# Norms on the residual rows in SBUF, operand splits woven between output projections, fewer DMAs: an attention and GLU block on one core

## The chip, the core and the metric

The kernel runs on one core of a Trainium2 chip. A core has a matrix engine (TensorE, PE, with its weight loads as PEld), a vector engine (VectorE, DVE), a scalar engine (ScalarE, ACT), GpSimd (POOL) and SyncE (SP), which here only issues DMAs. ACT issues DMAs too, in its own order of instructions. The metric is the device time of one execution in microseconds (us). What a measurement of this kernel can tell from no change is about 0.5%, some 4.4 us.

## What is computed

A block of batch 1, sequence 2048 and width 512: a conditioned layer norm, "infini" attention (32 heads of 16, four segments of 512 rows, each with causal softmax inside the segment and a linear-attention memory of the segments before), an output projection with residual, a second conditioned layer norm, and a bilinear GLU of width 1376 with residual:

```python
mod = silu(c) @ w_mod                      # six vectors: sa, ca, ga, sb, cb, gb
h = layernorm(x) * (1 + ca) + sa
q, k, v = heads(h @ wq), heads(h @ wk), heads(h @ wv)
for s in range(4):                         # segments of 512 rows
    p = softmax(q_s @ k_s.T * scale + mask)
    a_mem = phi(q_s) @ M / (phi(q_s) @ z + 1e-6)
    o_s = g * a_mem + (1 - g) * (p @ v_s)
    M, z = M + phi(k_s).T @ v_s, z + sum(phi(k_s))
x = x + ga * (concat(o) @ wo)
h = layernorm(x) * (1 + cb) + sb
out = x + gb * ((h @ w_gate) * (h @ w_up) @ w_down)
```

## The kernel before

**Stages.** The first 500 us are the attention. Its work is cut into 32 half-groups (one of four segments, four heads); `v` counts them, and a loop over `v` from -2 to 32 runs five slots in each step. In a slot stand, in the program's order: `q_step` (TensorE makes transposed scores `q`, and VectorE takes their maximum into `nm`, for the row maxima of a later step), in one slot `av_step` (exponentials times values, `tb`), `fill()`, and `k_step` (TensorE makes the scores `k`, ACT takes their exponential into `pt`, GpSimd zeroes what the mask excludes). The tile of scores is used again one slot later, so the scores of a slot wait for the exponential of the slot before. Once in a step `n_step` turns the maxima: they are transposed by TensorE (`ntp`), copied by VectorE to `nt` (32 rows of 128) and put by DMA on two spare rows of the query tile `qst`, so that the next step's scores come out with the maximum subtracted. Every VectorE instruction recorded by a wrapper has line 40, matmuls line 90, transposes line 93.

**The filling.** `fill()` advances generators that hold the work which is not scores: first `fill_a` (projections to queries, keys and values, the memory), then `fill_b`: the output projections of segments 0 to 2, the norm ahead of the GLU and the first GLU weights. A generator yields what it has put down; a credit of `rate * share` per slot stops the filling, and `yield False` ends the slot's filling at once. `weave(a, b, at)` advances `b` once after each listed step of `a`.

**Output projection.** Segment outputs were stored to HBM by an earlier stage (`od`, four groups of 128x512 per segment). `wo_load` loads them (tiles `orl`), `wo_op` splits each into a rounded part `oH` (ACT) and a rest, which stays in the `orl` tile (VectorE). `wo_mm` makes, for each 128-row tile of the segment, twelve matmuls (`wops`: high, rest and weight rest for four groups) and `wo_add` adds them to the residual rows `xr`, which `xr_load` has loaded, and stores the sum to HBM (`x1d`). `lnC` loads the sums again (`x<-x1d`), takes the norm (`bn_stats`, mean and variance, one `tensor_scalar` per tile) and transposes them (`ctp`) into what the GLU reads. The product of the GLU's weights is prepared by `prep`: loads of w_gate and w_up (tile `w`), sums on GpSimd, a rounded part `AH` by ACT and a rest `AL`.

**What sets the order.** TensorE and VectorE take the program's order here. ACT's and SP's order comes from the tile scheduler; SP issues one DMA after another, and one that waits for a buffer or for an earlier transfer holds all behind it. After 544 us comes the GLU, in two halves of the rows.

Of the kernel before, what the change touches and what calls it, by code (L numbers as in the profile page):

```python
# [9 lines left out]
F32 = mybir.dt.float32  # L10
# [8 lines left out]
P = 128  # L19
# [39 lines left out]
def tile_kernel(ctx, tc, x, wq, wk_, wv, wo, beta, w_gate, w_up, w_down, c, w_mod, out):  # L59
# [147 lines left out]
    def ln(pool, hpool, xt, s, sc, sh, pfx, hb, fast, kept_h=None):  # L207
# [5 lines left out]
        for d in range(KT):  # L213
            h = pool.tile([P, L], F32, tag="hf", name=f"{pfx}hf{s}_{d}", bufs=hb[2])
            ln_col(bank(f"{pfx}tp{s}_{d}"), h, xt, d, sc, sh, A)
            hi = hpool.tile([P, L], F32R, tag=hb[0].format(d), name=f"{pfx}hH{s}_{d}", bufs=hb[1])
            lo = hpool.tile([P, L], F32R, tag=hb[0].format(4 + d), name=f"{pfx}hL{s}_{d}", bufs=hb[1])
            if fast:
                V.tensor_copy(hi, h)
                V.tensor_sub(lo, h, hi.bitcast(F32))  # L220
            else:
                act.activation(hi, h, AF.Copy)
                nc.gpsimd.tensor_sub(lo, h, hi.bitcast(F32))  # L223
            hH.append(hi)
            hL.append(lo)
            if kept_h is not None:
                kept_h.append(h)
            yield 0.45
            if not first and d % 2 == 1:
                yield False  # L230
# [71 lines left out]
    def n_step(u):  # L302
# [6 lines left out]
        for i in range(2):  # L309
            nc.scalar.dma_start(Q[96 + i:97 + i].rearrange("p h (q t) -> p (h q) t", t=P), nt[16 * i:16 * i + 16])  # L310
# [116 lines left out]
    def prep(i, key, pool, nb, rpool, rb, ce=nc.gpsimd, le=nc.gpsimd, step=False):  # L427
# [3 lines left out]
        for src, k0, j in ((w_gate, 0, 0), (w_gate, 2, 1), (w_up, 0, 7), (w_up, 2, 2)):  # L431
            pin(nc.sync.dma_start(w[:, j, :, 0:n], src.rearrange("(k p) f -> p k f", p=P)[:, k0:k0 + 2, f0:f0 + n]))
# [34 lines left out]
    def wo_load(s, pool):  # L467
        rw = []
        for g in range(NG - 2 if s == NSEG - 1 else NG):
            a = pool.tile([P, L], F32, tag="orl", name=f"orl{s}_{g}", bufs=4)  # L470
            pin(nc.sync.dma_start(a, od[s][g]))
            rw.append(a)
        return rw
# [24 lines left out]
    def both(a, b):  # L498
        while True:
            x, y = next(a, None), next(b, None)  # L500
            if x is None and y is None:
                return
            yield 0.0

    def paced(a):
        for _ in a:
            yield False

    def xr_load(s, pb, ts=range(4), tag="xr"):
        xrs = []  # L510
        for t in ts:
            xr = pb.tile([P, D], F32, tag=tag, name=f"xr{s}_{t}", bufs=4)
            pin(nc.sync.dma_start(xr, x[rows(s, t), :]))
            xrs.append(xr)
        return xrs
# [13 lines left out]
    def wo_mm(s, us, xrs, ts=range(4)):  # L529

        for t, xr in zip(ts, xrs):
            ps = bank(f"wops{s}_{t}")
            yield from wo_row(ps, t, us, range(NG))
            wo_add(s, t, xr, ps)

    def lnC(s, pool, hpool, xpool, tag, nb):
        xt = []
        for t in range(4):
            a = xpool.tile([P, D], F32, tag=tag, name=f"x1_{s}_{t}", bufs=nb)
            nc.sync.dma_start(a, x1d[s][t])  # L540
            xt.append(a)
        yield 0.1
# [4 lines left out]
        for d in (0, 2, 1, 3):  # L547
# [3 lines left out]
            if d > 1:  # L551
                yield False
# [367 lines left out]
    us = [[], [], []]  # L920

# [33 lines left out]
    def fill_a():  # L955
# [5 lines left out]
        for s in range(NSEG):  # L961
# [4 lines left out]
            for g in range(2 if s == 0 else 0, NG):  # L966
# [17 lines left out]
                if s == NSEG - 1 and g == 1:  # L984
                    xr0 = xr_load(0, pa, (0, 1), "x")
# [3 lines left out]
                if s == NSEG - 1 and g == NG - 1:  # L989
                    yield from weave(Q, ready, (0, 1, 2, 3))  # L990
                    memq.append(a_mem(s, g))
# [121 lines left out]
    for v in range(-2, NQ + 1):  # L1113
        rate[0] = 5.8 if v < 20 else 5.2
        on, prev = 0 <= v < NQ, 0 <= v - 1 < NQ
        for slot in range(5):
# [10 lines left out]
            if v == NQ and slot == 0:  # L1127
                assert B["orl_free"]
                o3 = wo_load(3, B["pb"])
                xr3 = xr_load(3, B["pb"])  # L1130
            if v == NQ and slot == 2:
                btag[:] = ["ms", "lq0", "ms", "lq1"]
                for f in (fa, fb):
                    for _ in f:
                        pass
                us3 = []
# [162 lines left out]
    for q in range(2):  # L1299
# [42 lines left out]
        if q == 0:  # L1342
            def rows_of(s, tags):
                r = []
                for t, (tg, nb) in enumerate(tags):
                    a = wpool.tile([P, D], F32, tag=tg, name=f"xn{s}_{t}", bufs=nb)
# [6 lines left out]
            def norms():  # L1353
                for s, tags in ((2, [("orl", 4)] * 4), (3, [("wor", 2)] * 2 + [("orow", 2)] * 2)):
# [156 lines left out]
```

## Time and profile before

| | |
|---|---|
| time, median of 3 runs (least to most) | 879.39 us (879.31 to 883.21) |
| the profiled execution: its own time, its span | 881.91 us, 879.8 us |
| TensorE busy | 832.8 us (95%) |
| VectorE busy | 650.6 us (74%) |
| ACT busy | 472.5 us (54%) |
| GpSimd busy | 424.1 us (48%) |
| moved by DMA | 139.46 MB, 159 GB/s over the span |

The span runs from the first to the last recorded instruction; the execution's own time holds some 2 us around it. In a row of the timeline stand start, duration, engine, line, operation, tiles and shapes, and in brackets the idle time before it on its engine with what ended that. In a table of stretches stand, for each, the busy time and count of every engine, then the granted TensorE clock (1.00 is full), the busy share of the DMA engines and their rate. "ACTq" and "SPq" are the issue queues of ACT and SP.

### The profile page before, as it was taken

How to read it: one execution, taken by the hardware profiler on the slowest of the kernel's cores; microseconds unless marked ns; L12 is line 12 of the kernel's file. 1: busy time of each engine (PE TensorE's matmuls, PEld its weight loads, DVE VectorE, ACT ScalarE, POOL GpSimd, SP SyncE). 2: the span in 40 equal slices, each digit the busy share in tenths (PEclk: the TensorE clock that was granted, in tenths of full speed). 3: DMA queues.
4: the chain of work that ended last, by engine and by line, in shares of the span. 5: the costliest groups of instructions: out<-in, count | busy, mean ns of one | idle time of the engine just before them, and what ended most of it. 6: DMA issues, size and time to landing. Idle time of an engine off the chain costs nothing.

```text
span 879.8 us, 14406 instructions
## 1 busy us (share of the span) xinstructions
PE 832.8 (95%) x4824; PEld 583.0 (66%) x4824; DVE 650.6 (74%) x1728; ACT 472.5 (54%) x740; POOL 424.1 (48%) x564
## 2 busy tenths in 40 slices
PE   8998999989999989999978899999999999999998
PEld 5765565555565656655644567788778888887886
DVE  7697677986778868788888759898784856666532
ACT  3757667777677766777554664333363523333321
POOL 4545546546455665486352533987200846550000
PEclk9999899999999999999999999999999999999999
DMA  7774456665648665677695552543414232212032
GB/s 236 225 235 159 146 160 201 214 209 174 207 142 252 199 190 157 220 234 239 209 285 177 160 180 97 176 146 105 163 30 127 87 120 64 56 55 93 0 118 96
DMA packets 112667, 139.46 MB, mean 159 GB/s; under 512 B 20112, under 2 KB 71312, under 8 KB 112592
## 3 DMA queue, kind: packets, MB, share of 16 engines
q1 hardware_dynamic: 106368, 130.91, 48.7%
q10 hardware_dynamic: 6224, 7.62, 2.4%
q8 instruction: 38, 0.62, 0.3%
q14 instruction: 37, 0.30, 0.1%
HBM read 87.48 MB, written 50.76 MB: 157 GB/s over the span
## 4 chain that ended last, share of the span: by engine, by line
PE 66%; DVE 13%; DMA 8%; ACT 5%; POOL 4%; issue 3%; ACTq 1%; SPq 0%; POOLq 0%; DVEq 0%
PE g L90 23%; PE acc L90 14%; PE tb L90 5%; DVE q L40 5%; PE k L90 5%; PE q L90 5%; PE vps L90 4%; PE kps L90 3%; PE qps L90 2%; ACT pt L330 2%; DMA xr<-in_x_dram 2%; PE wops L90 2%; POOL ahL L223 1%; DVE x L40 1%; DVE nm L40 1%
## 5 line engine op out<-in xcount | busy, mean ns | idle before, releaser
L40 DVE CUSTOM_DVE_ANT_0 q<-q,cmask 128x384 f32<-128x384 f32 (+3 forms) x512 | 246.7, 508 | 66.4 <-PE q L90 56.4
L330 ACT ACTIVATE pt<-k 128x1024 f32<-128x1024 f32 x160 | 163.8, 1024 | 68.7 <-PE k L90 47.3
L333 POOL TENSOR_SCALAR_AFFINE_SELECT pt<-pt 128x256 f32<-128x256 f32 (+1 forms) x224 | 105.4, 484 | 174.3 <-ACT pt L330 173.9
L90 PE MATMUL q<-kst,qst 96*128 96x384 bf16 (+3 forms) x512 | 102.1, 301 | 11.7 <-DVE nm L40 10.4
L90 PE MATMUL k<-qst,kst 98*128 98x384 bf16 (+3 forms) x512 | 97.9, 303 | 11.6 <-ACT pt L330 10.7
L448 POOL TENSOR_TENSOR w<-w 128x256 f32<-128x256 f32 (+1 forms) x84 | 72.0, 869 | 55.7 <-DMA w<-in_w_up_dram 38.2
L443 POOL TENSOR_TENSOR AL<-w,AH 128x512 fp32r<-128x512 f32 (+1 forms) x42 | 58.2, 1388 | 48.0 <-ACT AH L439 46.8
L90 PE MATMUL tb<-pt,v 128*32 128x512 f32 (+3 forms) x1024 | 76.2, 438 | 0.2 <-POOL pt L333 0.2
L90 PEld LDWEIGHTS <-kst 98*128 98x128 bf16 x512 | 38.8, 99 | 56.6 <-issue 48.4
L40 DVE DVE_READ_ACCUMULATOR2_ANT nm<- 128x1 f32 x512 | 72.3, 141 | 0.0
L90 PEld LDWEIGHTS <-qst 96*128 96x128 bf16 x512 | 43.6, 98 | 39.1 <-issue 14.4
L439 ACT ACTIVATE AH<-w 128x512 fp32r<-128x512 f32 (+3 forms) x88 | 46.8, 565 | 33.6 <-POOL w L448 20.5
L1453 DVE TENSOR_TENSOR mL<-mid,mH 128x512 fp32r<-128x512 f32 (+1 forms) x44 | 32.9, 751 | 41.4 <-ACT mH L1452 39.4
L90 PE MATMUL acc<-DH,mL 128*128 128x512 f32 x144 | 56.6, 393 | 0.9 <-DVE mL L1453 0.9
L90 PE MATMUL acc<-DH,mH 128*128 128x512 f32 x144 | 57.2, 397 | 0.0
L90 PE MATMUL acc<-DL,mH 128*128 128x512 f32 x144 | 56.5, 393 | 0.0
L90 PEld LDWEIGHTS tb<-pt,v 128*32 128x32 f32 x1024 | 28.7, 110 | 39.5 <-issue 35.9
L1452 ACT ACTIVATE mH<-mid 128x512 fp32r<-128x512 f32 (+1 forms) x44 | 27.1, 627 | 51.7 <-PE acc L90 50.1
L1245 ACT ACTIVATE p<-g 128x512 f32<-128x512 f32 (+1 forms) x22 | 13.1, 597 | 73.2 <-PE g L90 73.1
L443 DVE TENSOR_TENSOR AL<-w,AH 128x512 fp32r<-128x512 f32 (+3 forms) x44 | 29.2, 671 | 19.1 <-ACT AH L439 18.2
L359 ACT ACTIVATE tsb<-tb 128x512 f32<-128x512 f32 x32 | 19.1, 596 | 35.0 <-PE tb L90 33.4
L90 PE MATMUL g<-chH,AH 128*128 128x512 f32 (+1 forms) x88 | 34.8, 395 | 0.7 <-ACT p L1245 0.7
(286 smaller groups left out, 2060.1 us busy)
## 6 DMA issues: line engine op xcount, KB each, us to landing
kst<-kd SPq DMA_DIRECT2D x32, 384.0 KB
qst<-qd SPq DMA_DIRECT2D x32, 384.0 KB
td<-tsb ACTq DMA_DIRECT2D x28, 256.0 KB
wm<-in_w_mod_dram SPq DMA_DIRECT2D x24, 256.0 KB
kd<-k SPq DMA_DIRECT2D x16, 384.0 KB
qd<-q SPq DMA_DIRECT2D x16, 384.0 KB
w<-in_w_gate_dram SPq DMA_DIRECT2D x40, 128.0 KB
w<-in_w_up_dram SPq DMA_DIRECT2D x40, 128.0 KB
```

Source lines behind the costliest of these rows:

```text
L40: i = getattr(self.eng, name)(*a, **k)
L90: return pe(nc.tensor.matmul(*a, **k))
L223: nc.gpsimd.tensor_sub(lo, h, hi.bitcast(F32))
L330: lpt[0] = act.activation(pt, kp, AF.Exp, scale=0.25)
L333: sels[u, i] = nc.gpsimd.affine_select(w, w, pattern=[[0, w.shape[1]], [1, P]], compare_op=ALU.is_ge, fill=0.0, base=0, channel_multiplier=-1)
L359: act.activation(tsbs[u], tbs.pop(u), AF.Copy)
L439: i = act.activation(hi[sl], w[sl], AF.Copy)
L443: i = eng.tensor_sub(lo[sl], w[sl], hi[sl].bitcast(F32))
L448: i = ce.tensor_tensor(w[:, o, :, 0:n], w[:, x, :, 0:n], w[:, y, :, 0:n], op=op)
L1245: lcp[0] = act.activation(r["p1"], ps, AF.Copy)
L1452: pin(act.activation(mH[0:n], md[0:n], AF.Copy))
L1453: vec.tensor_sub(mL[0:n], md[0:n], mH[0:n].bitcast(F32))
```

## The change

1. `n_step` puts both halves of `nt` on `qst` with one DMA (2x16x128) in place of two (1x16x128).
2. `prep` loads w_gate with one DMA for all four slices, not two.
3. `wo_load` loads a segment's outputs into one tile with one DMA (128x4x512, 1 MB); one such tile per pool rather than four small ones.
4. `xr_load` loads two row tiles at a time. The first two of segment 0 go to another pool than the one of the attention's inputs.
5. `lnC` no longer loads `x1d`: the norm works in place on `xr` once the sum is stored. The `bn_stats` of segment 1 are taken inside its output projection, each after its tile's addition.
6. `fill_b` is woven anew: the transposes `ctp` and the splits of the next segment stand between the matmuls of an output projection, the first `prep` moves behind the split of segment 2, the pauses of the norm (`yield False`) are gone, and the rate after step 20 is 5.1 and not 5.2. The generators are emptied in slot 0 of the last step, before the loads of segment 3, and not in slot 2.

```diff
@@ n_step
-        for i in range(2):
-            nc.scalar.dma_start(Q[96 + i:97 + i].rearrange("p h (q t) -> p (h q) t", t=P), nt[16 * i:16 * i + 16])
+        nc.scalar.dma_start(Q[96:98].rearrange("p h (q t) -> p (h q) t", t=P), nt)
@@ prep
-        for src, k0, j in ((w_gate, 0, 0), (w_gate, 2, 1), (w_up, 0, 7), (w_up, 2, 2)):
+        for src, k0, nk, j in ((w_gate, 0, 4, 0), (w_up, 0, 2, 14), (w_up, 2, 2, 4)):
@@
     def wo_load(s, pool):
-        rw = []
-        for g in range(NG - 2 if s == NSEG - 1 else NG):
-            a = pool.tile([P, L], F32, tag="orl", name=f"orl{s}_{g}", bufs=4)
-            pin(nc.sync.dma_start(a, od[s][g]))
+        n = NG - 2 if s == NSEG - 1 else NG
+        a = pool.tile([P, NG, L], F32, tag="orl", name=f"orl{s}", bufs=1)
+        pin(nc.sync.dma_start(a[:, 0:n], od[s][0:n].rearrange("g p t -> p g t")))
@@
-    def wo_mm(s, us, xrs, ts=range(4)):
+    def wo_mm(s, us, xrs, ts=range(4), norm=iter(())):
...
-            wo_add(s, t, xr, ps)
-
-    def lnC(s, pool, hpool, xpool, tag, nb):
-        xt = []
-        for t in range(4):
-            a = xpool.tile([P, D], F32, tag=tag, name=f"x1_{s}_{t}", bufs=nb)
-            nc.sync.dma_start(a, x1d[s][t])
-            xt.append(a)
-        yield 0.1
+            wo_add(s, t, xrs[t], ps)
+            if t < NG - 1:
+                next(norm, None)
+
+    def lnC(s, pool, hpool, xt):
@@ fill_b
-        rest = wo_mm(0, us[0], xr_load(0, pb, (2, 3)), (2, 3))
+        xr0.extend(xr_load(0, 2, pb, "xr"))
         o1 = wo_load(1, pb)
+        lg = kept_as("nxt", lnC(0, pb, bc, xr0))
+        rest = weave(wo_mm(0, us[0], xr0, (2, 3)), wo_op(1, pb, o1, us[1]), (4, 5, 5, 6, 6, 7, 7, 7))
+        yield from weave(rest, lg, (1, 2, 6))
+        B["o0"] = True
+        xr1 = xr_load(1, 0, pb, "x1") + xr_load(1, 2, pb, "x1")
         pr = prep(0, "0_0", bc, 1, pb, 1)
-        next(pr)
-        yield from weave(rest, wo_op(1, pb, o1, us[1]), (3, 4, 4, 5, 5, 6, 6, 7))
-        B["o0"] = True
-        lg = lnC(0, pb, bc, pb, "x1", 4)
-        yield from weave(wo_mm(1, us[1], xr_load(1, pb)), chain(pr, islice(lg, 10)), (0, 1, 2, 3, 4, 6, 7, 8, 9, 10, 11, 12, 13, 14))
+        lh = kept_as("hf", lnC(1, pb, bc, xr1))
+        rest = weave(wo_mm(1, us[1], xr1, range(4), lh), lg, (0, 1, 4, 5, 6, 7, 9, 11, 13, 15))
+        op2 = third(pb)
+        rest = weave(rest, op2, (10, 11, 12, 13, 14, 15, 16, 17))
+        yield from weave(rest, pr, (3,))
+        yield from lg
         while "o2" not in B:
             yield None
-        yield from weave(kept_as("nxt", lg), wo_op(2, pb, B["o2"], us[2]), (0, 0, 1, 1, 2, 2, 3, 3))
-        B["orl_free"] = True
-        lg = lnC(1, pb, bc, pb, "x1", 4)
-        yield from weave(wo_mm(2, us[2], xr_load(2, pb)), lg, (0, 1, 2, 3, 4, 5, 6, 7, 8, 9))
-        B["hf"] = yield from lg
+        yield from op2
+        xr2 = xr_load(2, 0, pb, "xr") + xr_load(2, 2, pb, "xr")
+        rest = weave(wo_mm(2, us[2], xr2), lh, (0, 1, 4, 5, 6, 7, 9, 11, 13, 15))
+        yield from weave(rest, pr, (2, 6, 11, 14))
+        yield from lh
@@ the loop over v
-        rate[0] = 5.8 if v < 20 else 5.2
+        rate[0] = 5.8 if v < 20 else 5.1
```

How the rows move, at three places. On ACT, steps 27 and 28, where the splits `oH` stand among the exponentials `pt` (`qst<-nt` is the DMA of the maxima, `AH` the split of GLU weights). Before:

```order
L492 ACTIVATE oH_0_5741<-orl_0_5655 128x512
L492 ACTIVATE oH_1_5750<-orl_1_5657 128x512
L330 ACTIVATE pt_0_5758<-k_0_5755 128x1024
L492 ACTIVATE oH_2_5813<-orl_2_5659 128x512
L492 ACTIVATE oH_3_5819<-orl_3_5661 128x512
L359 ACTIVATE tsb_5788<-tb_5771 128x512
L330 ACTIVATE pt_1_5796<-k_1_5793 128x1024
L361 DMA td_169<-tsb_5788 128x512
L439 ACTIVATE AH_0_5865<-w_0_5663 128x512
L330 ACTIVATE pt_2_5829<-k_2_5824 128x1024
L310 DMA qst_228<-nt_5835 1x16x128 x2
L330 ACTIVATE pt_3_5879<-k_3_5874 128x1024
```

Now, step 27 to the first exponential of step 28:

```order
L329 ACTIVATE pt_0_5710<-k_0_5707 128x1024
L490 ACTIVATE oH_0_5764<-orl_5644 128x512
L490 ACTIVATE oH_1_5770<-orl_5644 128x512
L490 ACTIVATE oH_2_5804<-orl_5644 128x512
L490 ACTIVATE oH_3_5810<-orl_5644 128x512
L358 ACTIVATE tsb_5740<-tb_5723 128x512
L329 ACTIVATE pt_1_5748<-k_1_5745 128x1024
```

```order
L329 ACTIVATE pt_4_5866<-k_4_5861 128x1024
L490 ACTIVATE oH_0_6053<-orl_5839 128x512
L490 ACTIVATE oH_1_6116<-orl_5839 128x512
L490 ACTIVATE oH_2_6164<-orl_5839 128x512
L181 ACTIVATE csd_5847<-cmv_5670,epst 128x4
L183 ACTIVATE cy_5849<-csd_5847 128x4
L329 ACTIVATE pt_0_5901<-k_0_5898 128x1024
```

In step 27 the first exponential now stands ahead of all four splits of segment 1; in step 28 three splits of segment 2 (tile 5839) stand ahead of the first exponential, where before it was one.

On SP, the loads of segments 1 and 2 (`x1d<-xr` is the store of a sum, `w` the GLU weights). Before:

```order
L527 DMA x1d_1_186<-xr_1_4674 128x512
L513 DMA xr_2_5651<-in_x_dram 128x512
L513 DMA xr_3_5653<-in_x_dram 128x512
L471 DMA orl_0_5655<-od_140 128x512
L471 DMA orl_1_5657<-od_140 128x512
L471 DMA orl_2_5659<-od_140 128x512
L471 DMA orl_3_5661<-od_140 128x512
L432 DMA w_0_5663<-in_w_gate_dram 128x2x128 x2
L432 DMA w_0_5663<-in_w_up_dram 128x2x128 x2
```

Now:

```order
L503 DMA xr_2_5642<-in_x_dram 128x2x512
L470 DMA orl_5644<-od_140 128x4x512
L516 DMA x1d_1_186<-xr_1_5317 128x512
L265 DMA kst_226<-kd_3_122 96x2048
L265 DMA qst_230<-qd_3_106 96x2048
L398 DMA rd_5575<-td_168 128x1x16
L399 DMA orow_5574<-td_168 64x1x512
L516 DMA x1d_2_187<-xr_2_5642 128x512
L420 DMA od_141<-orow_5227 128x512
L503 DMA xr_0_5815<-in_x_dram 128x2x512
L503 DMA xr_2_5817<-in_x_dram 128x2x512
L470 DMA orl_5839<-od_141 128x4x512
```

The load of segment 1 (od_140) goes ahead of the second store, and that of segment 2 (od_141) stands behind the four residual tiles of segment 1.

On VectorE, the norm of segment 0 among the score maxima (`ISA`) of steps 28 and 29. Before, on the reloaded tiles `x`:

```order
L40 ISA nm_6002 128x1
L40 TENSOR_SCALAR x_0_0_5938<-x_0_0_5938,cmv_6012,cy_6084 128x512
L40 TENSOR_TENSOR xr_2_5857<-xr_2_5857,wops_2_6049 128x512
L40 TENSOR_SCALAR x_0_1_5940<-x_0_1_5940,cmv_6012,cy_6084 128x512
L40 ISA q_4_0_6131,nm_6002<-q_4_0_6131,cmask 128x256
```

Now, on the residual tiles `xr`, with the `bn_stats` of segment 1 behind its addition:

```order
L40 ISA nm_5951 128x1
L40 TENSOR_SCALAR xr_2_5642<-xr_2_5642,cmv_5670,cy_5849 128x512 x2
L40 TENSOR_TENSOR xr_0_5815<-xr_0_5815,wops_1_5894 128x512
L40 BN_STATS cst_1_5997<-xr_0_5815 128x6
L40 BN_AGGR cmv_5890<-cst_1_5997 128x2
L40 ISA q_2_0_6013,nm_5951<-q_2_0_6013,cmask 128x512
```

The norm of segment 0 stands over half a step earlier, and that of segment 1 begins among the same maxima.

More of the change, by code (lines that the diff above doesn't have):

```diff
@@ L228, in ln @@
             yield 0.45
-            if not first and d % 2 == 1:
+            if pfx == "a" and not first and d % 2 == 1:
                 yield False
@@ L496, in wo_op, with xr_load @@
             yield 0.0
[L498 to L515, printed above, removed]
+    def xr_load(s, t, pool, tag):
+        if pool is wpool:
+            xr = [pool.tile([P, D], F32, tag=tag, name=f"xr{s}_{t + i}", bufs=2) for i in range(2)]
+            for i in range(2):
+                pin(nc.sync.dma_start(xr[i], x[rows(s, t + i), :]))
+            return xr
+        xr = pool.tile([P, 2, D], F32, tag=tag, name=f"xr{s}_{t}", bufs=2)
+        pin(nc.sync.dma_start(xr, x[s * L + t * P:s * L + (t + 2) * P, :].rearrange("(a p) d -> p a d", p=P)))
+        return [xr[:, 0], xr[:, 1]]
     def wo_row(ps, t, us, gs, late=False):
@@ L1344, in rows_of @@
                 r = []
-                for t, (tg, nb) in enumerate(tags):
-                    a = wpool.tile([P, D], F32, tag=tg, name=f"xn{s}_{t}", bufs=nb)
+                if tags:
+                    b = wpool.tile([P, NG, D], F32, tag="orl", name=f"xn{s}", bufs=1)
+                for t in range(4):
+                    if tags:
+                        a = b[:, t]
+                    else:
+                        a = wpool.tile([P, D], F32, tag=("wor", "orow")[t // 2], name=f"xn{s}_{t}", bufs=2)
                     pin(nc.sync.dma_start(a, x1d[s][t]))
@@ L1353, in norms @@
             def norms():
-                for s, tags in ((2, [("orl", 4)] * 4), (3, [("wor", 2)] * 2 + [("orow", 2)] * 2)):
+                for s, tags in ((2, "orl"), (3, None)):
                     xn[s] = rows_of(s, tags)
```

26 lines of the change are left out of this document (14 added, 12 removed).

## The prediction

> **What bounds the kernel now.** I read the page's busy shares first, then the table of stretches, and then the waits and the timeline of the one stretch that stood out.
>
> ```profile
> PE 832.8 (95%) x4824; PEld 583.0 (66%) x4824; DVE 650.6 (74%) x1728; ACT 472.5 (54%) x740; POOL 424.1 (48%) x564
> core 0: us, PE busy (x) PEld busy (x) DVE busy (x) ACT busy (x) POOL busy (x), PEclk, DMA share, GB/s
> 348.00:439.00 91.00, 87.07 (x627) 53.11 (x626) 75.36 (x267) 61.24 (x88) 52.03 (x72) 1.00 0.72 227
> 439.00:500.00 61.00, 49.36 (x336) 29.37 (x335) 50.53 (x165) 32.17 (x45) 27.78 (x42) 0.97 0.69 208
> 544.00:850.00 306.00, 304.59 (x1334) 244.62 (x1333) 214.06 (x312) 113.67 (x209) 140.22 (x139) 1.00 0.33 99
> 450.00:460.00 10.00, 7.57 (x42) 4.91 (x40) 8.26 (x24) 4.86 (x8) 8.54 (x12) 1.00 0.95 311
> 460.00:470.00 10.00, 8.35 (x63) 4.67 (x64) 7.35 (x29) 4.90 (x7) 1.26 (x3) 1.00 0.97 282
> 485.00:490.00 5.00, 3.38 (x14) 2.33 (x15) 3.08 (x11) 3.74 (x6) 1.43 (x2) 0.70 0.40 117
> ```
>
> TensorE is the bound: the change takes no matmul away, so it can only win idle time of TensorE. From 544 us to 850 us there is none to win (304.59 us busy of 306). The stretch in which the first output projections are woven into the last score steps, 439 to 500 us, is the opposite: 49.36 us busy of 61, so 11.6 us idle, while the stretch ahead of it loses 3.9 us in 91. The whole case is decided in these 61 us. Their idle time, by what ended it (engine, line, releaser: us, times, longest), and its largest pieces on TensorE:
>
> ```profile
> PE k L90 <- ACT pt L330: 6.1, 4, 2.3
> PE q L90 <- DVE nm L40: 3.3, 6, 0.9
> PE ctp L93 <- DVE x L40: 1.4, 1, 1.4
> PE k L90 <- DMA qst<-nt: 0.4, 1, 0.4
> 447.65 0.59 PE L90 MATMUL k<-qst,kst 98*128 98x512 bf16 x2 [2.28 <-ACT pt L330]
> 457.38 0.60 PE L90 MATMUL k<-qst,kst 98*128 98x256 bf16 x4 [2.26 <-ACT pt L330]
> 460.30 0.60 PE L90 MATMUL k<-qst,kst 98*128 98x512 bf16 x2 [0.43 <-DMA qst<-nt]
> 467.34 0.60 PE L90 MATMUL k<-qst,kst 98*128 98x384 bf16 x4 [1.35 <-ACT pt L330]
> ```
>
> Up to 470 us the scores `k` wait for the exponentials of the step before, and after it the transposed scores `q` wait for maxima `nm`. ACT is not busy when it is late; its own timeline and that of SP, which issues the loads, say why:
>
> ```profile
> 435.91 0.34 SPq L527 DMA_DIRECT2D x1d<-xr  x1
> 439.91 0.81 SPq L513 DMA_DIRECT2D xr<-in_x_dram  x2
> 440.78 1.84 SPq L471 DMA_DIRECT2D orl<-od  x4
> 444.79 0.63 ACT L492 ACTIVATE oH<-orl 128x512 fp32r<-128x512 f32 x1 [3.36 <-DMA orl<-od]
> ...
> 450.78 1.03 ACT L330 ACTIVATE pt<-k 128x1024 f32<-128x1024 f32 x1 [0.23 <-POOL pt L333]
> 451.18 0.21 DVE L40 COPY nt<-ntp 32x128 bf16<-32x128 bf16 x1
> 454.31 1.90 ACTq L310 DMA_DIRECT2D qst<-nt  x2
> 456.31 1.02 ACT L330 ACTIVATE pt<-k 128x1024 f32<-128x1024 f32 x1 [4.50 <-DVE nm L40]
> 459.46 0.85 SPq L471 DMA_DIRECT2D orl<-od  x2
> 465.26 0.63 ACT L492 ACTIVATE oH<-orl 128x512 fp32r<-128x512 f32 x1 [2.43 <-DMA orl<-od]
> ```
>
> Twice a split `oH` stands in ACT's order ahead of an exponential and waits for its load (3.36 and 2.43 us), and once the two `qst<-nt` issues stand there: their row was copied by 451.39 us, but the issues came at 454.31. The releaser named for the exponential behind them (nm) had long been done, so I read this as a wait for earlier transfers, in a stretch where the DMA engines are busy 0.95.
>
> **The change part by part.** The sum is made against the profiled execution's own 881.91 us (span 879.8), which lies 2.5 us above the median of 879.39; the forecast takes these 2.5 us off again. Four more rows for points 1 to 4, from the list of DMA issues and the timelines:
>
> ```profile
> x<-x1d SPq DMA_DIRECT2D x8, 256.0 KB
> ...
> 504.70 0.30 ACT L181 ACTIVATE csd<-cmv,epst 128x4 f32<-128x4 f32 x1 [0.30 <-DVE cmv L40]
> 470.27 0.60 PE L90 MATMUL k<-qst,kst 98*128 98x384 bf16 x4 [0.18 <-ACT pt L330]
> 501.28 0.21 DVE L40 COPY nt<-ntp 32x128 bf16<-32x128 bf16 x1 [1.18 <-PE ntp L93]
> ```
>
> 1. The load of segment 1's outputs goes earlier and becomes one DMA. Before, SP issued a store at 435.91 and got to the next load only at 439.91: 4.0 us in which it waited until an `xr` buffer was free, and the loads `orl<-od` stood behind it. With the first two `xr` tiles in another pool nothing of that is left. ACT's order now has the exponential ahead of the four `oH`, which come in a row: 4 x 0.63 = 2.5 us, before the next exponential. So 2.28 us go, at worst all of it stays as a wait for those four; I leave 0.5 us: **-1.8** (bounds 0 and -2.3).
>
> 2. The wait of the `qst<-nt` issues. In the crowded 20 us the change takes out the four rereads of segment 0's rows (4 x 256 KB) and moves the first GLU weights behind the split loads; two issues become one. I take **-2.0** of the 2.26 (bounds 0 and -2.26: the queue may still be full of the new 1 MB pieces).
>
> 3. The split of segment 2. Its load is one 1 MB DMA in place of four, issued where the last matmul of the first output projection has been made, which stands just ahead of the fourth score step of step 27: the third exponential was at 450.78 and ends 1.03 later, less the 2.28 of point 1, so about 449.5 us. Ahead of it in the queue are 1 MB of `xr` rows: 2 MB at the 282 to 311 GB/s of the rows above are 6.7 to 7.4 us, so it lands at about 457. Behind it ACT has three `oH` (1.9 us), two small operations (0.5, an estimate from a `csd` of 0.30 us) and then the first exponential of step 28 (1.0): scores can go on at 460.4. They are wanted at about 459 (the scores of step 28 started at 460.30, less 2.28 and 2.26 is 455.8, and a fifth of a step later, of 16.7 us, a third of what lies between the two `nt` copies, 451.18 and 501.28). So 1.4 us of stall stand against 0.43 + 1.35 + 0.18 before: **-0.6** (bounds -2.0 and, if the DMA lands with the last piece of before, at 465.26, +7.7).
>
> VectorE's operations in this stretch (count | busy us, mean ns of one | idle before), and the stretches that follow the two above:
>
> ```profile
> L40 DVE TENSOR_TENSOR orl<-orl,oH 128x512 fp32r<-128x512 f32 x7 | 6.1, 890 | 0.0
> L40 DVE TENSOR_TENSOR xr<-xr,wops 128x512 f32<-128x512 f32 x5 | 3.4, 673 | 0.0
> L40 DVE BATCH_NORM_STATS2 cst<-x 128x6 f32<-128x512 f32 x4 | 2.7, 687 | 0.0
> L40 DVE TENSOR_SCALAR x<-x,cmv,cy 128x512 f32<-128x512 f32 x4 | 2.1, 531 | 0.5 <-POOL cy L191 0.5
> L40 DVE TENSOR_TENSOR AL<-w,AH 128x512 fp32r<-128x512 f32 (+1 forms) x2 | 1.3, 626 | 1.6 <-ACT AH L439 1.6
> ...
> 470.00:480.00 10.00, 8.33 (x65) 4.70 (x64) 8.81 (x26) 3.68 (x6) 5.25 (x12) 1.00 0.29 92
> 480.00:490.00 10.00, 7.84 (x44) 4.71 (x37) 7.91 (x31) 6.36 (x9) 2.43 (x4) 0.85 0.39 124
> 490.00:500.00 10.00, 8.60 (x69) 5.40 (x69) 9.69 (x31) 6.11 (x10) 6.76 (x7) 0.98 0.74 191
> ```
>
> 4. The waits for VectorE, 3.3 + 1.4 = 4.7 us. No VectorE operation is taken away. Between the same two copies `nt` (451.18 and 501.28 before) its list is the same but for two subtractions `orl` (2 x 0.890) in place of two `AL` (1.3): 0.5 us more. In 450 to 500 us VectorE was busy 42.0 us (8.26 + 7.35 in the rows above, 26.4 in the rest) and TensorE 40.7: the two are nearly even, so a smoother order can win from both, but VectorE must not be idle for it. The norm's operations still come in lumps: two `tensor_scalar`, an add and a `bn_stats` in a row (2 x 0.531 + 0.673 + 0.687 = 2.4 us) ahead of a score maximum. **-0.8** (bounds 0 and -4.7).
>
> 5. The granted clock was 0.70 from 485 to 490 us, right after the gaps. 3.38 us of matmuls at full clock would be 1.0 us less; most gaps of its kind stay: **-0.3** (bounds 0 and -1.0).
>
> The issues of `qst<-nt` (duration ns, least, median, most) and ACT's queue (packets, MB, share of 16 engines' span):
>
> ```profile
> L310 ACTq DMA_DIRECT2D qst<-nt x64: 510/531/1343, 53.1 to 502.1; - x64
> ...
> q10 hardware_dynamic: 6224, 7.62, 2.4%
> ```
>
> 6. One `qst<-nt` issue less in each of the 32 steps: 32 x 0.53 = 17 us of ACT's queue, hidden by ACT's idle 46% except where an exponential is late: **-0.2** (bounds 0 and -0.6, one issue in each of points 1 to 3 with no cover).
>
> 7. Costs: four `oH` in a row ahead of an exponential once more (segment 0, step 21), and the rest of the generators drained two slots earlier in the last step, ahead of what TensorE needs there: **+0.5** (bounds 0 and +2.5, the length of four `oH`).
>
> Half as many loads of w_gate and the paced pauses of the norm cost nothing: SP issues them, and nothing of 544 to 850 us waits for it. Sum: -1.8 -2.0 -0.6 -0.8 -0.3 -0.2 +0.5 = **-5.2**; 881.9 - 5.2 - 2.5 = **874.2 us**.
>
> **The rivals.** (a) VectorE takes the gain: it is busy 42.0 of 50 us and its idle time sits in the very stalls that go. Then points 2 to 5 turn into waits for maxima and only point 1 is left: 879.4 - 1.8 = 877.6 us. For it: the `q` waits from 470 us on; against it: nearly 8 us of idle VectorE.
> (b) Slower: the 1 MB load of segment 2 lands as one piece and late, and ACT stands with three `oH` ahead of the exponential that all scores need. Break-even is where its stall, landing + 3.4 - 459, less the 1.96 of before, eats the 4.6 us of the other terms: landing at 462.2. At 467 it is 11.4 us of stall: 9.4 - 4.6 = +4.8, so 884.2 us. For it: a piece issued at 459.46 was used at 465.26 in a queue that was 0.97 busy; against it: issued some 10 us earlier, with 1 MB less to reread.
> (c) The merged `qst<-nt` lands later than its halves did and the first scores of a step wait. Only one step of this stretch waited for it (0.4 us), but if its 32 rows go through two engines, 16 one after another on each, at the mean packet time of ACT's queue q10 (0.024 x 16 x 879.8 us / 6224 = 54 ns) it lands 15 x 54 ns = 0.8 us later; with a quarter of the steps tight that is +6.5: 880.7 us. The trace has no such DMA, so nothing in it tells whether this happens. The Trainium skill, "DMA: Bandwidth & Descriptors", section "Why a DMA increments its semaphore by 16 and not by 1", says that a DMA is spread over the largest number up to 16 that divides the slowest dimension of both sides that is not 1: by it this one, 2x16x128, runs on two engines and the old ones, 1x16x128, on sixteen, so that the page speaks against merging them; no run shown here can tell.
> (d) The weave does what it can: all 11.6 us but some 2 go, and the clock stays up (1.0): 881.9 - 10.6 - 2.5 = 868.8 us. For it: VectorE needs 42.0 of 50; against it: its list is no shorter.
>
> **How the numbers follow.** Forecast 0.40, (a) 0.27, (b) 0.10, (c) 0.09, (d) 0.14. The range goes from 867.5 (d, with its clock) to 881.5, which holds (a) and (c) and cuts most of (b). What a measurement of this kernel can tell from no change is 0.5%, 4.4 us: faster is below 875.0. The forecast's own spread is 871 to 877, two thirds of it below 875.0: 0.28, with (d) and a little of (a) 0.28 + 0.14 + 0.06 + (c's lighter end) 0.03 = 0.51 faster. Slower (above 883.8) is 0.07 of (b), 0.02 of (c) and 0.02 for what I have not seen: 0.11. The rest, 0.38, is no change that can be told.
>
> **What would show it.** In the changed profile the stall of some 2.3 us at the second score step of step 27 is gone, and ACT has no `oH` that waits 3 us. `qst<-nt` is issued within 1 us of its copy there. If (a) holds, the waits of `q` for `nm` grow past 6 us; if (b), ACT waits over 5 us in one `oH`; if (c), a group "k waits for DMA qst<-nt" of several us stands over all 32 steps. I am wrong from the ground up if the idle time moves to other stretches than 439 to 500 us.

## The result: slower, and the stretch that was forecast gained

The changed kernel takes 893.53 us (median of 4 runs, 891.61 to 895.62) against 881.3 us (median of 4) for the kernel before, run alongside: a ratio of 1.0129, 95% interval 1.0103 to 1.0154. It is slower by 1.3%; 874.2 us were forecast, with 867.5 to 881.5 as the range.

The page of the changed kernel: the span, the busy times, the chain of waits, and ACT's queue (packets, MB, share):

```profile
span 892.1 us, 14286 instructions
PE 841.2 (94%) x4824; PEld 585.9 (66%) x4824; DVE 654.1 (73%) x1728; ACT 475.8 (53%) x740; POOL 423.3 (47%) x564
PE 69%; DVE 13%; ACT 5%; DMA 5%; POOL 4%; issue 3%; SPq 0%; ACTq 0%; POOLq 0%; DVEq 0%
q10 hardware_dynamic: 5264, 7.62, 2.3%
```

TensorE runs the same 4824 matmuls in 841.2 us and not in 832.8: 8.4 of the 12.3 us between the two profiled executions are not idle time but slower matmuls, at a mean granted clock that the list of cores gives as 0.983, before as 0.992. The rest is idle time. To see where, both executions are cut at the same work: the start of steps 20, 23, 24, 27 and 31, and one fixed matmul at the GLU's start. The matmul counts of a piece agree within 4, so the lengths can be compared. The kernel before:

```profile
347.70:386.60 38.90, 38.04 (x274) 23.26 (x272) 31.18 (x112) 28.33 (x41) 23.05 (x32) 1.00 0.75 235
386.60:400.50 13.90, 12.85 (x92) 7.68 (x91) 12.07 (x43) 9.52 (x16) 9.56 (x13) 1.00 0.61 198
400.50:440.30 39.80, 37.72 (x275) 23.16 (x273) 33.45 (x120) 24.36 (x34) 19.99 (x32) 1.00 0.72 224
440.30:505.60 65.30, 53.71 (x362) 32.52 (x360) 52.69 (x170) 34.45 (x48) 29.17 (x47) 0.97 0.70 209
505.60:532.90 27.30, 26.33 (x178) 17.91 (x177) 16.48 (x29) 16.16 (x24) 8.96 (x16) 1.00 0.48 154
```

The changed kernel:

```profile
345.80:390.60 44.80, 40.27 (x270) 24.11 (x269) 30.25 (x112) 27.15 (x39) 19.01 (x28) 0.92 0.62 193
390.60:409.30 18.70, 14.58 (x92) 7.82 (x91) 14.74 (x41) 10.15 (x16) 13.19 (x15) 0.91 0.45 143
409.30:450.20 40.90, 38.54 (x274) 23.45 (x274) 33.56 (x120) 25.06 (x35) 21.65 (x33) 1.00 0.79 247
450.20:511.10 60.90, 53.42 (x362) 31.25 (x360) 51.10 (x168) 34.03 (x46) 25.06 (x46) 0.97 0.57 179
511.10:545.10 34.00, 29.12 (x182) 19.60 (x181) 17.89 (x31) 17.48 (x26) 10.95 (x17) 0.95 0.40 124
```

| piece | before | changed | difference |
|---|---|---|---|
| start to step 20 | 347.7 | 345.8 | -1.9 |
| steps 20 to 22 | 38.9 | 44.8 | +5.9 |
| step 23 | 13.9 | 18.7 | +4.8 |
| steps 24 to 26 | 39.8 | 40.9 | +1.1 |
| steps 27 to 30 | 65.3 | 60.9 | -4.4 |
| step 31 to the GLU | 27.3 | 34.0 | +6.7 |
| GLU to the end | 346.9 | 347.0 | +0.1 |

The piece on which the forecast rests, steps 27 to 30, gained 4.4 us of the 5.2 us forecast. The loss lies in three places outside it: steps 20 to 22, step 23, and the end of the attention. The four longest waits on TensorE from step 20 to the GLU, one in each of the three and one (454.12) in steps 27 to 30:

```profile
374.39 1.01 PE L90 MATMUL k<-qst,kst 98*128 98x256 bf16 x4 [3.48 <-ACT pt L329]
396.48 0.38 PE L90 MATMUL q<-kst,qst 96*128 96x256 bf16 x2 [3.58 <-DVE nm L40]
454.12 0.60 PE L90 MATMUL k<-qst,kst 98*128 98x512 bf16 x2 [2.00 <-DMA qst<-nt]
519.64 0.85 PE L93 MATMUL ctp<-ident,xr 128*128 128x128 f32 x4 [1.90 <-DVE xr L40]
```

**Steps 20 to 22.** The exponential that is waited for at 374.39 stood on ACT behind four splits `oH` of segment 0, and these behind their load (SP's and ACT's timeline):

```profile
358.86 1.82 SPq L265 DMA_DIRECT2D qst<-qd  x1
362.43 0.43 SPq L470 DMA_DIRECT2D orl<-od  x1
...
371.24 2.19 ACT L490 ACTIVATE oH<-orl 128x512 fp32r<-128x512 f32 x4 [3.47 <-DMA orl<-od]
373.34 1.00 ACT L329 ACTIVATE pt<-k 128x1024 f32<-128x1024 f32 x1
```

Before, the same load was issued at 354.39, in step 20 and ahead of the key and query loads of a later step:

```profile
354.39 2.00 SPq L471 DMA_DIRECT2D orl<-od  x4
```

So it is issued 8 us later in the profile, and 9.9 us later counted from the start of step 20 (16.6 us into it, not 6.7); its four `oH` stand in a row ahead of an exponential. What follows the stall of 3.48 us costs again: the granted clock falls to 0.50. It also falls behind the stalls at 396.48 and 454.12 (changed kernel, stretches of 5 us):

```profile
370.00:375.00 5.00, 1.52 (x8) 0.90 (x8) 0.60 (x2) 3.76 (x7) 2.60 (x3) 0.82 0.50 170
375.00:380.00 5.00, 5.00 (x19) 3.12 (x17) 3.34 (x10) 3.23 (x6) 3.62 (x5) 0.50 0.65 183
395.00:400.00 5.00, 3.00 (x16) 0.89 (x19) 4.90 (x15) 0.17 (x2) 5.00 (x5) 0.71 0.15 52
455.00:460.00 5.00, 5.00 (x39) 1.88 (x38) 2.27 (x11) 3.78 (x7) 0.41 (x1) 0.66 0.92 288
```

No part of the change names segment 0's load as moved. One part reaches it: the filling rate after step 20, 5.1 for 5.2. That is theory 1. Its rivals: the 1 MB load lands late wherever it stands (theory 2), and the norms in place and the new weave lose it (theory 3).

### The profile page after: what moved, and what is told of

It is laid out like the page before. It is cut to its first block, busy times and chain, and to the rows that moved or that the text cites. A ratio compares the mean times of both kernels' runs of the same rounds, so it can differ in the third digit from the quotient of the medians.

```text
span 892.1 us, 14286 instructions
## 1 busy us (share of the span) xinstructions
PE 841.2 (94%) x4824; PEld 585.9 (66%) x4824; DVE 654.1 (73%) x1728; ACT 475.8 (53%) x740; POOL 423.3 (47%) x564
## 3 DMA queue, kind: packets, MB, share of 16 engines
q10 hardware_dynamic: 5264, 7.62, 2.3%
## 4 chain that ended last, share of the span: by engine, by line
PE 69%; DVE 13%; ACT 5%; DMA 5%; POOL 4%; issue 3%; SPq 0%; ACTq 0%; POOLq 0%; DVEq 0%
PE g L90 23%; PE acc L90 14%; PE tb L90 7%; DVE q L40 6%; PE k L90 5%; PE q L90 5%; PE vps L90 4%; PE wops L90 3%; PE qps L90 2%; ACT pt L329 2%; PE kps L90 2%; PE up L90 1%; POOL ahL L223 1%; DMA orl<-od 1%; DVE nm L40 1%
## 5 line engine op out<-in xcount | busy, mean ns | idle before, releaser
L332 POOL TENSOR_SCALAR_AFFINE_SELECT pt<-pt 128x256 f32<-128x256 f32 (+1 forms) x224 | 103.2, 474 | 184.3 <-ACT pt L329 183.4
L90 PE MATMUL tb<-pt,v 128*32 128x512 f32 (+3 forms) x1024 | 79.1, 450 | 1.1 <-POOL pt L332 1.1
L90 PEld LDWEIGHTS <-kst 98*128 98x128 bf16 x512 | 38.9, 99 | 54.4 <-issue 45.5
L443 DVE TENSOR_TENSOR AL<-w,AH 128x512 fp32r<-128x512 f32 (+3 forms) x44 | 33.1, 753 | 14.5 <-ACT AH L439 13.7
```

The costliest lines, as they stand in the source:

```text
L90: return pe(nc.tensor.matmul(*a, **k))
L332: sels[u, i] = nc.gpsimd.affine_select(w, w, pattern=[[0, w.shape[1]], [1, P]], compare_op=ALU.is_ge, fill=0.0, base=0, channel_multiplier=-1)
L443: i = eng.tensor_sub(lo[sl], w[sl], hi[sl].bitcast(F32))
```

## The experiments

Every ratio is to the kernel before, run alongside, with its 95% interval. The lengths of pieces are those of one profiled execution of each kernel.

### The rate put back

```diff
-        rate[0] = 5.8 if v < 20 else 5.1
+        rate[0] = 5.8 if v < 20 else 5.2
```

> The changed kernel with the filling rate after step 20 put back from 5.1 to 5.2, all else as changed. Theory 1 (the rate): the smaller rate puts the load of segment 0's outputs from step 20 (issued at 354.4 us before) to step 21 (362.4), behind two query/key loads; its four oH then hold ACT 3.5 us ahead of an exponential, TensorE stalls 3.5 us, the granted clock falls to 0.50 and a second lump follows at 395 us. At 5.2 the load stands where it stood before, so some 9 to 11 us come back: 881 to 885 us, and no stall over 2 us in steps 21 to 23. Theory 2 (the one-piece load lands late wherever it is issued): stays at 890 or more, with ACT waiting over 2 us in an oH. Theory 3 (the norms in place and the new weave lose it): stays at 890 or more, without that wait.

Measured: 876.49 us, ratio 0.9939 (0.9917 to 0.9961): 0.6% faster than before, 5.4 us by that ratio, where the changed kernel was 1.3% slower. More came back than the 881 to 885 us expected: one digit of one number is worth 1.9%, some 17 us. Its pieces, cut at the same work:

```profile
348.20:387.20 39.00, 38.09 (x274) 23.31 (x272) 31.00 (x112) 28.16 (x42) 22.61 (x31) 1.00 0.69 219
387.20:401.30 14.10, 12.83 (x92) 7.68 (x91) 12.29 (x44) 9.27 (x15) 10.41 (x13) 1.00 0.62 197
401.30:442.40 41.10, 39.33 (x276) 24.09 (x274) 34.24 (x122) 24.52 (x34) 20.09 (x32) 0.96 0.80 246
442.40:502.00 59.60, 53.51 (x361) 31.75 (x360) 52.32 (x171) 33.97 (x46) 26.73 (x49) 0.97 0.58 183
502.00:530.40 28.40, 26.57 (x179) 18.07 (x178) 18.19 (x30) 17.17 (x26) 10.51 (x14) 1.00 0.49 148
```

Against the changed kernel: 39.0 for 44.8, 14.1 for 18.7, 28.4 for 34.0. All three losses come with the rate, and steps 27 to 30 keep their gain (59.6 for 65.3 before, -5.7). Theories 2 and 3 fall as the cause of the loss. A one-piece load that lands late is there all the same, in another place: in step 27 ACT waits for that of segment 1 (ACT's timeline at 5.2):

```profile
447.24 2.19 ACT L490 ACTIVATE oH<-orl 128x512 fp32r<-128x512 f32 x4 [3.76 <-DMA orl<-od]
```

### The rate alone, in the kernel before

```diff
-        rate[0] = 5.8 if v < 20 else 5.2
+        rate[0] = 5.8 if v < 20 else 5.1
```

> The kernel before with only the rate after step 20 changed, from 5.2 to 5.1. Theory 1: the same shift of segment 0's loads without any other part of the change, a wait of ACT in an oH in step 21 and a lower clock after it: 887 to 892 us. Theories 2 and 3: 879 to 883 us, as before.

Measured: 894.78 us, ratio 1.0167 (1.0118 to 1.0215), more than expected. With loads in four pieces and nothing else changed, the splits wait in step 21 and the scores behind them:

```profile
368.47 1.29 ACT L492 ACTIVATE oH<-orl 128x512 fp32r<-128x512 f32 x2 [1.97 <-DMA orl<-od]
371.72 0.60 PE L90 MATMUL k<-qst,kst 98*128 98x384 bf16 x4 [2.68 <-ACT pt L330]
```

The rate loses in either kernel. The rest of the change gains 0.6% at 5.2; at 5.1 its 1.0129 beside this 1.0167 is no difference that the intervals show, though the profile gains in steps 27 to 30 (60.9 us there, 66.2 us here, from 447.0 to 513.2).

### The one-piece load, alone and undone

In the kernel before, `wo_load` as in the change (one tile, one DMA); in the changed kernel, four DMAs into the one tile:

```diff
-        pin(nc.sync.dma_start(a[:, 0:n], od[s][0:n].rearrange("g p t -> p g t")))
+        for g in range(n):
+            pin(nc.sync.dma_start(a[:, g], od[s][g]))
```

> The kernel before with only the load of a segment's outputs made one DMA into one tile (and the last norms' rows in the matching tiles). Theory 2: ACT waits for the load of 1 MB in step 21, 28 or both, 884 to 890 us. Theory 1: step 21 is not touched, since the load is still issued in step 20; four oH stand in a row there (2.2 us), 879 to 883 us.

> The changed kernel, rate 5.1, with the load of a segment's outputs as four DMAs into its one tile. If the size of the one DMA makes the wait, ACT's wait in an oH of step 21 falls below 1.5 us and the time to 884 to 888. If it is the place of the load in SP's order (362 us), which stays, the wait stays at 2.5 us or more, and the time at 890 or more.

Alone it gave 883.51 us, 1.0029 (1.0002 to 1.0056), between the two expectations and less than can be told from no change. No `oH` waits in step 21, as theory 1 says, but theory 2 has a place too, in step 27, where the load of segment 1 stands late in the order of the kernel before. One piece, with all four `oH` behind it, makes ACT wait longer there than four (6.37 us, before 3.36; ACT's timeline of that kernel):

```profile
451.28 2.19 ACT L490 ACTIVATE oH<-orl 128x512 fp32r<-128x512 f32 x4 [6.37 <-DMA orl<-od]
```

Undone at rate 5.1 it gave 893.34 us, 1.0112 (1.0078 to 1.0146), no different from 1.0129. The time is the one expected if the place of the load makes the loss, but the wait in step 21 lies between the two expectations (ACT's timeline):

```profile
370.87 1.29 ACT L491 ACTIVATE oH<-orl 128x512 fp32r<-128x512 f32 x2 [2.16 <-DMA orl<-od]
```

In that profile steps 20 to 22 take 42.5 us (348.9 to 391.4), with one piece 44.8 and before 38.9. So the late issue makes most of the wait, and the one piece lengthens it; that this share reaches the time of the whole kernel is not shown.

### One DMA for the maxima, alone

The diff is that of the change's first part.

> The kernel before with only the two DMAs of the maxima per step made one. The changed kernel was 1.9 us ahead at step 20, where this is the only part of the change that can act; if that is so, 877 to 880 us. If the merged DMA lands later (two engines in place of sixteen) and steps wait for it: 881 us or more, with a group of waits of k for qst over the steps.

Measured: 881.17 us, 0.9983 (0.996 to 1.0005): no change that can be told, with 0.17% as the middle. Its profiled execution started step 20 at 345.2 us (before 347.7), but profiled starts of unchanged parts vary as much (348.2 and 345.6 in two executions of the changed kernel at other rates), so the early 1.9 us are not shown to be its work. No step waits for the merged DMA in the first 345 us of this kernel or of the changed one. So neither expectation is confirmed.

### The rate between 5.1 and 5.2, and above

A quantum is what a generator puts down between two yields.

> The changed kernel at rate 5.14, nearer to 5.1 than to 5.2. In the order of SP the load of segment 0's outputs stands at 5.14 where it stands at 5.2, and at 5.12 where it stands at 5.1. If the loss is that step, 5.14 gives 875 to 880 us. If it grows smoothly with a slower filling, it lies past the middle towards 5.1: 885 to 890.

> The changed kernel at rate 5.3. If 5.1 is a bad place by chance of where the quanta fall, and not the first of a slope, 5.3 lies near 5.2: 874 to 880 us. If the time follows the rate (filling late costs, early wins), it lies below 5.2: 866 to 873.

5.14 gave 882.92 us, 1.0012 (0.9995 to 1.003); 5.3 gave 877.52 us, 0.9948 (0.9919 to 0.9977). So 5.3 is as good as 5.2, and nothing more is won by filling that much faster. At 5.14 neither expectation held: the load of segment 0 stands early again and steps 20 to 23 are as at 5.2, but the end of the attention is as long as at 5.1 (step 31 to the span's end 381.1 us, at 5.1 381.0, at 5.2 375.4). It is as long by another wait: the longest there is 2.42 us of TensorE for GpSimd's mask of an exponential (506.00), not the one at 519.64 of the changed kernel. The time falls from 5.1 to 5.2 and is flat above; in the pieces it goes by jumps, and not all at one rate: at 5.14 the first loss is gone and the last is not.

### The load put down earlier

```diff
+                        B["orl"] = wo_load(0, wpool)
                         yield from a_v(s)
-                        B["orl"] = wo_load(0, wpool)
```

> The changed kernel, rate 5.1 kept, with one line moved: the load of segment 0's outputs is put down ahead of the value projections of the last segment, not behind them, so it is issued two steps earlier and its oH stand in step 19. If the late load and the four oH behind it are what the rate costs, the stall of 3.5 us in step 21 goes, its low clock too, and the time falls to about 880 to 884 us. If the rate costs by everything else that it moves (weight splits and memory work one quantum later, the stall of 3.6 us in step 23), 3 to 5 us come back at most: 887 to 891.

> The same moved line at rate 5.2. In the kernel at 5.2 no oH waits in step 21, so the line should be worth nothing there: 875 to 878 us. If four oH in a row ahead of an exponential cost there too, up to 2 us less.

At 5.1: 888.59 us, 1.008 (1.0053 to 1.0108). No `oH` waits in step 21 any more, as the first theory says, but the time is in the range of the second. Steps 20 to 22 are back at 39.3 us, so the late load was 5.5 of their 5.9 us; step 23 (19.5 us) and the end (some 381 us from step 31) stay long. At 5.2: 875.88 us, 0.9926 (0.9898 to 0.9953), not to be told from 0.9939. It is the fastest kernel of this study by its middle value.

Step 23 in the kernel at 5.1 with that line (timelines of ACT, VectorE and TensorE; `woH` is the rounded part of a slice of the output weights, `woL` the rest):

```profile
389.43 0.63 ACT L919 ACTIVATE woH<-wor 128x512 fp32r<-128x512 f32 x1
390.09 1.81 DVE L40 TENSOR_TENSOR woL<-wor,woH 128x512 fp32r<-128x512 f32 x1 [2.94 <-ACT woH L919]
...
392.88 0.58 PE L90 MATMUL q<-kst,qst 96*128 96x256 bf16 x2 [4.29 <-DVE nm L40]
```

At 5.2 the same subtraction stands at the same place of VectorE's order and waits for nothing:

```profile
387.95 0.89 DVE L40 TENSOR_TENSOR woL<-wor,woH 128x512 fp32r<-128x512 f32 x1
```

At 5.1 the last two slices of the output weights are loaded, scaled and split later (their loads are issued together at 379.58, where at 5.2 they stand at 375.81 and 378.04), but the subtraction's place among VectorE's maxima has not moved; four score maxima stand behind the subtraction, and TensorE behind those.

### Step 23: the subtraction moved out of the way

Two quanta later on VectorE, or on GpSimd, each with the hoisted load at 5.1:

```diff
-                     (scaled, 2), (halves, 2), (scaled, 3), (halves, 3)):
+                     (scaled, 2), (halves, 2), (scaled, 3), (None, 0), (None, 0), (halves, 3)):
```

```diff
-            (vec if k % 2 else nc.gpsimd).tensor_sub(lo, raw[k], hi.bitcast(F32))
+            (vec if k == 1 else nc.gpsimd).tensor_sub(lo, raw[k], hi.bitcast(F32))
```

> The changed kernel at 5.1 with the hoisted load, and in the weights' preparation the last split two quanta later, so that VectorE's subtraction woL stands behind four more score maxima of step 23. If the rest of the loss (888.6 against 876.5) is VectorE standing 2.9 us at woL ahead of the maxima while its split is late, the wait falls below 1 us and the time by 3 to 6: 882 to 886. If the stall of step 23 comes from the maxima alone or from slow VectorE operations beside a busy GpSimd, it stays: 887 to 890.

> The changed kernel at 5.1 with the hoisted load, and that last subtraction on GpSimd, not on VectorE. VectorE then waits for no split in step 23 at all. If that wait is the rest of the loss: 878 to 884. If GpSimd, which is busy there all the time, becomes late with the key and query rests instead, 886 or more, with waits behind GpSimd.

Measured: 884.17 us, 1.0041 (1.0019 to 1.0063), and 885.47 us, 1.006 (1.0037 to 1.0083), the latter above its 878 to 884 and below its 886. The first falls into its range, though VectorE still waits 1.12 us and not under 1: step 23 takes 17.2 us, where it took 19.5 and at 5.2 14.1, so somewhat under half of its loss comes back. The rest became a wait for GpSimd, which masks the exponentials (the first kernel, TensorE):

```profile
390.15 0.64 PE L90 MATMUL tb<-pt,v 128*32 128x256 f32 x8 [2.41 <-POOL pt L332]
```

GpSimd has the key and query rests, the weights and the masks in these 5 us, and is the next in line.

### The end: five small operations, and the rate from step 28

In the changed kernel segment 1's norm needs five 4-wide GpSimd operations for its inverse root. VectorE stood for the last of them, and the transposes behind it (VectorE's timeline of the changed kernel; TensorE's row is the one at 519.64 above):

```profile
516.38 1.00 DVE L40 TENSOR_SCALAR xr<-xr,cmv,cy 128x512 f32<-128x512 f32 x2 [5.80 <-POOL cy L191]
```

Moved to VectorE, at both rates:

```diff
-        eng = CV if first else nc.gpsimd
+        eng = CV if first else vec if (pfx, s) == ("c", 1) else nc.gpsimd
+        if (pfx, s) == ("c", 1):
+            yield 0.0
```

> The changed kernel at 5.1 with the hoisted load and the later weight split (884.2), and of segment 1's norm the five 4-wide operations of the inverse root on VectorE, not on GpSimd, one quantum later. In the changed kernel they took 8 us on GpSimd among its long operations, VectorE stood 5.8 us for the last of them, and the transposes of the end were late (511 to 545 us took 5.6 us longer than at 5.2). If that is the last part of the loss, the stretch from step 31 to the span's end falls from 381 to 375 to 377 us and the time to 878 to 880. If the end is longer for another reason (the generators emptied in one slot, the clock), it stays at 380 or more and the time at 883 or more.

> The same five operations on VectorE at rate 5.2 with the hoisted load (875.9 before this). There VectorE does not stand for them at the end, so it should be worth nothing: 874 to 878 us.

This failed: 889.22 us, 1.0094 (1.0057 to 1.0131), where 884.17 us, 1.0041, stood without it, and 881.84 us, 1.0009 (0.9985 to 1.0033), where 875.88 us, 0.9926, stood at 5.2. At 5.1 the intervals still touch; at 5.2 it is a loss. From step 31 to the span's end it is some 384 us at 5.1, above 380 as expected if the end is long for another reason. VectorE's wait for the root is gone, but SP now issues the last segment's load behind one more store of a sum, 17.2 us into step 31 for 15.7 (at 5.2 14.5 for 9.5): its `oH` now wait, and the last output projection behind them (the kernel at 5.1):

```profile
526.65 0.50 PE L90 MATMUL wops<-woH,oH 128*128 128x512 f32 x1 [2.74 <-ACT oH L492]
```

So I changed the rate at the end alone:

```diff
-        rate[0] = 5.8 if v < 20 else 5.1
+        rate[0] = 5.8 if v < 20 else 5.1 if v < 28 else 5.4
```

> The changed kernel with the hoisted load, rate 5.1 up to step 27 and 5.4 from step 28, so that the filling catches up and the transposes, the additions and the norm of segment 1 stand at the end where rate 5.2 puts them; steps 20 to 27 are as at 5.1 (888.6 us with the hoisted load). If the 5.6 us of the end are the price of arriving there one quantum late, the stretch from step 31 to the span's end falls from 381 to about 375 and the time to 881 to 884. If they are not, it stays at 887 or more.

Measured: 884.03 us, 1.0003 (0.9972 to 1.0035), at the upper end of what was expected. Step 31 to the GLU is 28.6 us again (34.0 in the changed kernel, 28.4 at 5.2), while step 23 stays at 19.5:

```profile
388.10:407.60 19.50, 15.15 (x92) 8.25 (x91) 14.11 (x41) 10.35 (x16) 13.67 (x16) 0.82 0.42 137
506.90:535.50 28.60, 26.75 (x179) 18.08 (x178) 19.02 (x30) 17.11 (x26) 10.25 (x13) 1.00 0.49 147
```

So with the rate raised from step 28 the 5.6 us of the end go: they are the price of getting there late with the filling. In the rows of the changed kernel and of 5.2, 3.05 us of them are idle time (34.00 - 29.12 against 28.40 - 26.57), and 2.55 us busy time, at a clock of 0.95 for 1.00 and with three more matmuls. Which wait begins it, the root's or one that the emptied generators bring, these runs leave open: at 5.14 the end is as long with another wait, and removing the root's alone did not bring the time back.

Within their intervals of some 0.3% the parts add up: 1.0129 as changed, 1.008 with the load earlier, 1.0003 with the end's rate too. What is left to 0.9939 is 0.64%, 5.6 us, and step 23's 19.5 for 14.1 us is 5.4.

## Why the prediction was wrong, point by point

**The step that failed** is the one that confined the case: "The whole case is decided in these 61 us." It took TensorE's idle time before as all that could be won, and, but for point 7 and rival (c), did not ask what could be lost where TensorE was busy. In the working, point 7 is the term: "four `oH` in a row ahead of an exponential once more (segment 0, step 21)", +0.5, bounds 0 and +2.5. It saw the four rows move on ACT and priced their length. It did not look where SP issues the load they wait for: behind two more loads, 8 us later. That place measured +5.9 us, clock included, and issuing the load earlier took back 5.5. The rate, 5.1 for 5.2, got no term of its own. It moves every later quantum of the filling; step 23 (+4.8) and the end (+6.7) were not in the sum at all, and the second half of point 7, the earlier emptying, was given a share of the same +0.5. The prediction's own last sign came: the idle time moved to other stretches than 439 to 500 us. And ACT has an `oH` that waits 3 us, which it ruled out (3.47 us, step 21). Slower had been given a chance of 0.11.

**Points 1 to 4 (-1.8, -2.0, -0.6, -0.8).** Their sum, 5.2 us, was near for their place: steps 27 to 30 gained 4.4 us in the changed kernel and 5.7 at rate 5.2. Piece by piece it was mixed, so that the sum came so near is in part luck. At 5.1 the stall of point 1 is gone; at 5.2 the four `oH` wait (3.76 us on ACT) and leave 1.9 us of it (the waits of steps 27 to 30 on TensorE, rate 5.2):

```profile
PE q L90 <- DVE nm L40: 2.2, 6, 0.9
PE k L90 <- ACT pt L329: 1.9, 1, 1.9
PE wops L90 <- ACT chf L205: 0.9, 1, 0.9
PE k L90 <- DMA qst<-nt: 0.6, 1, 0.6
PE ctp L93 <- DVE xr L40: 0.5, 1, 0.5
```

Point 2's stall went in both, but in the changed kernel the maxima of the step before came late: their DMA was issued at 446.34, behind the load of segment 1 at 445.50, and `k` waited 2.00 us for it, until 454.12. Point 3's wait for segment 2's load did not come. Of point 4's 4.7 us, 2.2 + 0.5 are left at 5.2, more than the 0.8 forecast came back.

**Point 5** was the wrong way round for the kernel: the clock was costed as -0.3 in one place, but TensorE was busy 8.4 us longer over the kernel, 6.8 of it in the three pieces that lost. Each of the four longest stalls has a stretch of low clock behind it (0.50, 0.71, 0.66 and, from 519.6 to 525, 0.68).

**Point 6** (-0.2): the merged DMA measured 0.17% less time, with an interval that holds zero.

**The rivals.** (b) had the right mechanism at the wrong place: a 1 MB load that comes late with `oH` ahead of an exponential, but segment 0's in step 21, not segment 2's in step 28, and with its place in SP's order, more than the one piece, as the cause. (a), maxima that take the gain, did not decide: in steps 27 to 30 the waits for maxima fell (3.3 us before, 2.6 in the changed kernel, 2.2 at 5.2). (c), the merged DMA landing later, did not show as a wait of k over all steps: the changed kernel has one, the 2.00 us at 454.12, and the kernel before one of 0.43 us. Whether the merge or the 1 MB load issued just ahead makes it late is not shown; with that load in four pieces at 5.1 there is no such wait. ACT's queue has 960 packets fewer (6224 to 5264), 30 per step, so that two are left of 32. That agrees with a DMA on two engines, as the Trainium skill has it ("DMA: Bandwidth & Descriptors", section "Why a DMA increments its semaphore by 16 and not by 1"); but the two are not 16 small packets each in a row, as the price of (c) assumed, and alone the merge lost no time that can be told. (d) did not come.

The range missed the time by 12 us on its upper side. With the rate left at 5.2 the kernel measured 876.49 us, 2.3 us above the forecast, and gained 5.4 us where 5.2 were forecast. The 2.3 us are the 2.5 that the forecast took off for a profiled execution above its median: that median came from three runs, and in the later runs the medians of the kernel before are 880.9 to 882.4 us, so its 881.9 was no slow one. That 5.4 meets 5.2 is luck in part too: the profiled execution at 5.2 gained 5.7 us in steps 27 to 30 and gave back 1.3 in steps 24 to 26 and 1.1 at the end, which no term names; it is 879.09 us, only 2.8 less than the 881.91 of before.

## What to carry to other kernels

A pacing number is a change like any other: list which instructions it moves on every engine and queue, over the whole stretch in which it holds, before costing the parts that the change talks about. Where the new order has an instruction with others queued behind it, look up on the issuing queue when the load it waits for is now issued. And cost a new stall of 2 to 4 us on the bounding engine at more than its length, since behind most of them here the clock fell.

## What the runs showed of the hardware

- A stall of 3.48 us on TensorE was followed by at least 5 us at a granted clock of 0.50, one of 3.58 us by 0.71 over the next 5 us. Stalls of 2.00 and 1.90 us (454.12 and 519.64) were followed by 0.66 and 0.68 over some 5 us. But in the kernel before two stalls of 2.3 us, at 445 and 455 us, left it at 1.00, and so did one of 2.68 us (371.72) in that kernel at rate 5.1. So length alone does not decide; what does is not shown.
- The subtraction woL took 1.81 us in step 23 at rate 5.1 and 0.89 us at 5.2. In the first case GpSimd had a subtraction of its own that starts at the same 390.09 and takes 1.26 us:

```profile
390.09 1.26 POOL L920 TENSOR_TENSOR woL<-wor,woH 128x512 fp32r<-128x512 f32 x1
391.31 1.70 POOL L418 TENSOR_TENSOR orow<-orow,memb 128x512 f32<-128x512 f32 x1
```

The Trainium skill, "SBUF — State Buffer", section "Who interferes with whom", says that VectorE and GpSimd share one pair of ports as an exclusive lock. The rows agree with it, and no run here separates it from other causes. That GpSimd works beside VectorE does not lengthen it by itself: the same kernel's other woL on VectorE, at 374.62, took 0.69 us, and GpSimd started an operation 0.05 us after it.
